# Linear attention into a two-expert mixture: places packed without a gap, and one tile at run-time offsets

## The chip, the cores and the metric

The kernel runs on one core of a Trainium2 chip. The metric is the device time of one execution in microseconds. Five engines work side by side on that core: TensorE (PE in the profile, PEld for its weight loads), VectorE (DVE), ScalarE (ACT), GpSimd (POOL) and SyncE (SP, which only issues transfers). The names PEq, PEldq, DVEq and so on are the instruction sequencers of these engines.

## What is computed

The reference, cut to what matters (8 batches, 8 heads, 576 tokens each, head width 64; so N = 4608 rows of D = 512; 8 experts with F = 1024; 2 modalities):

```python
q_s = softmax(q, axis=-1);  k_s = softmax(k, axis=2)
kv  = einsum('bhsd,bhse->bhde', k_s, v)
x   = einsum('bhsd,bhde->bhse', q_s, kv)      # then as N rows of D
logits = x @ w_gate + modality_bias[modality_id]
e_idx  = argmax(logits, axis=1)
gate_w = softmax(logits)[e_idx]
for e in range(E):
    mask = e_idx == e
    h = maximum(x[mask] @ w1[e], 0.0)
    out[mask] = gate_w[mask, None] * (h @ w2[e])
```

The inputs are one fixed draw. In it 2277 rows have modality 0 and 2331 have modality 1, and the expert that a row's argmax chooses is the one that its modality's bias favours.

## The kernel before

**Two experts are loaded, and rows are sorted by modality.** The kernel reads from the bias which expert each modality favours and loads the weights of these two alone into `W[:, 0]` and `W[:, 1]` (side A and side B). For each batch it loads q, k and v into a ring of five buffers `st`, takes exponentials (ACT), sums (DVE, L761), normalises q (mostly POOL, L777), builds `kv` on PE (L888) and from it a block-diagonal `kvbd` (DVE, L924), transposes q into the order of modalities on PE by a permutation matrix (L956, "s1"; the matrix `perm` comes from DVE, L806), multiplies by `kvbd` (L995, "s2"), and then copies windows of 64 columns into their places in `xs` (L1026, a "put", 18 of them per batch, on ACT, or on DVE for batches 2 and 5). Where a window starts is read at run time from running counts (`aoff`).

**Places.** `xs` holds NSLOT = 4864 places, 38 tiles of 128. Side A fills them from the left and side B from the right, each with up to CAP = 2432 places (19 tiles), so a gap is left between them. `lst`, `has` and `idx` hold the output row of each place, and `has` whether there is one.

**Passes.** For each side, seven passes run over fixed ranges of places (`passes_a`; `passes_b` mirrors them). A pass with number n may begin when batches 0 to n of its side have been put. Its widths are 256, 256, 256, 256, 512, 512 and 384 places. A pass computes the gates (logits on PE, L1060; bias and maximum on DVE, L1071 and L1072; exponentials on ACT, L1076), then for each of 8 blocks f of the hidden layer four matmuls (L1117, `h_mm`) and a relu (DVE L1093 or ACT L1091), and then for each tile eight matmuls of 512 columns (L1127, `y_mm`), a scaling by the gate (DVE L1099 or ACT L1097), and an indirect store of 128 rows on POOL (L1102).

**What sets the order.** A planner in the program (`Plan`) writes the instruction order of every engine ahead of time: a list scheduler with a cost and a rank for every step and rings of buffers (`r_ps` for seven PSUM banks, `r_st` for the loads). It runs at build time, so any step that is added, dropped or priced anew can shift the order of others. Up to 32 us it fills PE's gaps with matmuls that nothing reads (L1224).

**The general path.** After the planned part, `keys()` (L1240 to L1244) finds the expert of each place, a matmul counts the places whose expert is the expected one, and `ok` compares the running counts with what the passes assumed. If all hold, `nrest` is 0 and every engine skips a loop over all experts (branch at L1286, loop end at L1373) which would recompute everything. With this draw it is skipped. Its body begins with the logits and gates of all 38 tiles, so on PE it is long.

Of the kernel before, what the change touches and what calls it, by code (L numbers as in the profile page):

```python
# [232 lines left out]
def kernel(  # L233
# [44 lines left out]
    xs = sb([P, KD, NSLOT], BF16, "xs")  # L278
# [43 lines left out]
    def consts_pool(_):  # L322
# [11 lines left out]
        g.iota(kt_i, pattern=[[-64, NC]], base=NSLOT - 64, channel_multiplier=0)  # L334
# [281 lines left out]
    def vals_run(_):  # L616
# [4 lines left out]
        d.tensor_scalar(out=vals[:, :, 1], in0=idl, scalar1=1.0, scalar2=None, op0=ALU.add)  # L621

    def bsel_run(_):
# [5 lines left out]
        d.tensor_tensor(out=bsel, in0=bsel, in1=view(bias_b, [[0, NSL], [1, E]]), op=ALU.add)  # L629

# [53 lines left out]
    def idx_run(_):  # L684
# [27 lines left out]
    o_bsel = pl.op({"DVE": (1.17, 1.27, True)}, bsel_run, [o_off, o_exp], rank=11.5)  # L712
# [12 lines left out]
    def window(at, of_pass, T, last, right):  # L725

        lo, w = of_pass[1], of_pass[2]
        off = lo + (w - T) // 2
        if last:
            off = (lo if right else lo + w) - T // 2  # L730
# [3 lines left out]
            ap=[list(xs.ap[0]), [NSLOT, KD], [1, T]],  # L734
# [643 lines left out]
```

## Time and profile before

| | before |
|---|---|
| median of 3 runs | 215.15 us (214.55 to 215.34) |
| the profiled execution's own time | 213.42 us |
| its span in the profile | 211.7 us |
| mean granted TensorE clock | 0.974 of full speed |
| PE busy | 185.2 us (87%) |
| DVE busy | 155.4 us (73%) |
| ACT busy | 114.6 us (54%) |
| POOL busy | 97.2 us (46%) |

The time around the span is 213.42 - 211.7 = 1.72 us. The profiled execution lies 1.73 us below the median of the runs. Spans in the sections that follow are positions in the profiled execution, from the start of its span.

### The profile page before, as it was taken

Reading aid. Unit: us, or ns where it says so; the run is one execution under the profiler, and the core shown is the slowest. Engines: PE = TensorE matmul, PEld = TensorE weight load, DVE = VectorE, ACT = ScalarE, POOL = GpSimd, SP = SyncE. Lnnn points to the kernel's source line nnn. Section 1 sums busy time; section 2 is a strip of 40 time slices with the busy share of each in tenths; the row PEclk is TensorE's granted clock in tenths of the full one; section 3 lists DMA queues with packets and bytes.
Section 4 is the critical chain, followed back from the end, with each engine's and each line's share of the span. In section 5 each row is a group of like instructions: output and inputs, shape, how many; then the busy total and the mean of one; then the engine's idle time right before and its main releaser. Section 6 shows DMA issues by size and latency. Waiting matters only on the chain.

```text
span 211.7 us, 4660 instructions
## 1 busy us (share of the span) xinstructions
PE 185.2 (87%) x1587; PEld 110.4 (52%) x1587; DVE 155.4 (73%) x380; ACT 114.6 (54%) x313; POOL 97.2 (46%) x114
## 2 busy tenths in 40 slices
PE   3577959898978999999986999999999999999930
PEld 1234448487546585867653555554444444555520
DVE  3699798977679997887899977559757465566530
ACT  3528958989458599999797279959000000000000
POOL 3041950946933499767814937240150330505140
PEclk9999988999999999999999799999999999999996
DMA  6899999999999997999696100130031130312030
GB/s 193 290 398 392 212 184 215 281 370 297 292 412 411 403 397 229 366 374 376 186 405 249 50 3 0 51 125 29 0 150 51 50 148 0 149 53 89 0 116 5
DMA packets 20299, 42.35 MB, mean 200 GB/s; under 512 B 2607, under 2 KB 4655, under 8 KB 20272
## 3 DMA queue, kind: packets, MB, share of 16 engines
q1 hardware_dynamic: 13296, 28.33, 36.9%
q0 software_dynamic: 6304, 13.64, 23.2%
q8 instruction: 14, 0.23, 0.5%
q10 hardware_dynamic: 672, 0.05, 0.2%
q14 instruction: 13, 0.11, 0.2%
HBM read 36.76 MB, written 9.96 MB: 221 GB/s over the span
## 4 chain that ended last, share of the span: by engine, by line
PE 54%; DMA 21%; ACT 6%; DVE 6%; POOL 3%; issue 3%; SPq 2%; ACTq 0%; DVEq 0%; POOLq 0%
PE ps L1127 25%; PE ps L1117 23%; DMA W<-in_moe_w_dram 8%; DMA wg_f<-in_moe_w_gate_dram 5%; DMA st<-in_k_dram 4%; DMA st<-in_v_dram 4%; PE ps L956 2%; PE ps L888 2%; PE ps L1060 2%; ACT xs L1026 2%; ACT hT L1091 2%; PE ps L995 1%; ACT ex L1076 1%; DVE eq L777 1%; DVE own L761 1%
## 5 line engine op out<-in xcount | busy, mean ns | idle before, releaser
L1117 PE MATMUL ps<-xs,W 128*128 128x256 bf16 (+2 forms) x448 | 74.1, 317 | 1.9 <-ACT hT L1091 0.8
L1127 PE MATMUL ps<-W,hT 128*128 128x512 bf16 (+1 forms) x312 | 69.3, 374 | 1.8 <-DMA W<-in_moe_w_dram 1.2
L1102 POOL DMA_INDIRECT out_dram<-y_sb,idx x38 | 37.6, 990 | 68.9 <-DVE y_sb L1099 63.6
L1117 PEld LDWEIGHTS <-W 128*128 128x128 bf16 x448 | 43.4, 99 | 25.2 <-issue 4.9
L1127 PEld LDWEIGHTS <-hT 128*128 128x128 bf16 x312 | 30.0, 98 | 33.3 <-issue 2.1
L1099 DVE TENSOR_SCALAR y_sb<-ps,gate 128x512 f32<-128x512 f32 (+1 forms) x35 | 25.7, 734 | 27.2 <-PE ps L1127 23.5
L1093 DVE TENSOR_SCALAR hT<-ps 128x512 bf16<-128x512 f32 (+2 forms) x62 | 35.2, 576 | 7.0 <-PE ps L1117 4.9
L1026 ACT CAST xs<-ps 128x256 f32 (+1 forms) x108 | 32.8, 473 | 0.2 <-PE ps L995 0.2
L777 POOL TENSOR_TENSOR eq<-st,qi 128x512 bf16<-128x512 f32 (+1 forms) x30 | 28.3, 973 | 6.3 <-issue 3.2
L798 POOL CAST vb<-st 128x1152 bf16<-128x1152 f32 x14 | 15.8, 1146 | 18.5 <-DMA st<-in_v_dram 16.8
L761 DVE TENSOR_REDUCE own<-st 128x18 f32<-128x1152 f32 x16 | 21.6, 1352 | 2.9 <-ACT st L755 2.6
L755 ACT ACTIVATE st<-st 128x1152 f32<-128x1152 f32 x16 | 18.1, 1160 | 5.1 <-DMA st<-in_q_dram 5.1
L968 ACT CAST et<-ps 128x512 bf16<-128x512 f32 (+1 forms) x26 | 14.1, 573 | 12.1 <-PE ps L956 9.1
L1091 ACT ACTIVATE hT<-ps 128x256 bf16<-128x256 f32 (+1 forms) x50 | 18.7, 420 | 2.9 <-PE ps L1117 2.8
L788 ACT ACTIVATE ek<-st 128x1152 bf16<-128x1152 f32 x16 | 18.5, 1184 | 2.7 <-DMA st<-in_k_dram 2.7
L1076 ACT ACTIVATE ex<-L,gmx 128x8 f32<-128x8 f32 x38 | 11.5, 303 | 7.7 <-DVE gmx L1072 6.9
L956 PE MATMUL ps<-perm,eq 128*128 128x128 bf16 x144 | 13.6, 229 | 2.2 <-DVE eq L777 2.0
L888 PE MATMUL ps<-vb,ek 64*128 64x129 bf16 x288 | 11.4, 217 | 4.5 <-POOL vb L798 2.9
L1224 PE MATMUL ps<-ones 128*128 128x512 bf16 x43 | 13.5, 473 | 1.2 <-POOL ones L324 1.2
L888 PEld LDWEIGHTS <-ek 64*128 64x128 bf16 x288 | 8.7, 93 | 9.4 <-issue 7.0
L956 PEld LDWEIGHTS <-eq 128*128 128x128 bf16 x144 | 9.9, 102 | 6.6 <-DVE eq L777 3.0
L1026 DVE CAST xs<-ps 128x256 f32 x36 | 12.2, 417 | 0.0
(106 smaller groups left out, 142.1 us busy)
## 6 DMA issues: line engine op xcount, KB each, us to landing
st<-in_q_dram SPq DMA_DIRECT2D x7, 1152.0 KB, 11.4
st<-in_k_dram SPq DMA_DIRECT2D x7, 1152.0 KB, 13.8
st<-in_v_dram SPq DMA_DIRECT2D x7, 1152.0 KB, 10.4
W<-in_moe_w_dram POOLq DMA_DIRECT2D x8, 256.0 KB
W<-in_moe_w_dram POOLq DMA_DIRECT2D x4, 512.0 KB
st<-in_q_dram SPq DMA_DIRECT2D x2, 576.0 KB, 5.8
st<-in_k_dram SPq DMA_DIRECT2D x2, 576.0 KB, 8.1
st<-in_v_dram SPq DMA_DIRECT2D x2, 576.0 KB
```

What stands on the lines that cost most here:

```text
L761: nc.vector.tensor_reduce(out=sums[qib.idx][:, h * NJ : (h + n) * NJ], in_=view(st[bq.idx], [[Dh, n * NJ], [1, Dh]], h * NJ * Dh), op=ALU.add,
L777: (nc.vector if e == "DVE" else nc.gpsimd).tensor_tensor(out=view(eq[eqb.idx], [[HG * Dh, n], [Dh, HG], [1, Dh]], j0 * HG * Dh), in0=view( ...
L788: nc.scalar.activation(out=view(ek[ekb.idx], [[Dh, n], [HG * Dh, NJ], [1, Dh]], h * Dh), in_=view(st[bk.idx], [[NJ * Dh, n], [Dh, NJ], [1, ...
L888: nc.tensor.matmul(out=ps_t[kvp[hg].idx][:, 130 * hp : 130 * hp + 129], lhsT=ek[ekb.idx][rows, j, P * hp : P * hp + P], rhs=vb[vbb.idx][ro ...
L956: nc.tensor.matmul(out=view(t, [[2 * nj * 64, 2], [1, 64]], hp * nj * 64 + jj * 64), lhsT=eq[eqb.idx][:, j0 + jj, P * hp : P * hp + P], rh ...
L1026: w_ = nc.scalar.copy(out=dst, in_=src) if e == "ACT" else nc.vector.tensor_copy(out=dst, in_=src)
L1091: nc.scalar.activation(out=dst, in_=src, func=ACT.Relu)
L1093: nc.vector.tensor_scalar_max(out=dst, in0=src, scalar1=0.0)
L1099: nc.vector.tensor_scalar(out=dst, in0=src, scalar1=g, scalar2=None, op0=ALU.mult)
L1102: s_ = nc.gpsimd.indirect_dma_start(out=out, out_offset=bass.IndirectOffsetOnAxis(ap=ix[:, c : c + 1], axis=0), in_=ysb, in_offset=None, b ...
L1117: nc.tensor.matmul(out=t[:, 0:w], lhsT=W[:, slot_, kd * F + f * P : kd * F + (f + 1) * P], rhs=xs[:, kd, lo : lo + w], start=(kd == 0), st ...
L1127: nc.tensor.matmul(out=t, lhsT=h[:, kf, i * P : (i + 1) * P], rhs=W[:, slot_, W2 + kf * D + c0 : W2 + kf * D + c0 + cn], start=(kf == 0), ...
```

## The change

Places are packed: `xs` has exactly N = 4608 places, 36 tiles, with no gap; the middle is MID = 2304, after 18 tiles. The fixed passes cover 18 tiles on each side, the last one with 256 places instead of 384. The tile in which the larger side runs over the middle holds rows of both sides; the fixed pass of the smaller side's expert runs over it too, and the rows of the wrong side there get an output index out of bounds. One more tile, the **rest**, goes over it again with the larger side's expert (`ffn_rest`). Which tile it is and which expert is known only at run time: `mid_run` (DVE) computes `over`, the patched indices and `idx_x`; ACT reads two registers (`load_at`), copies the tile out of `xs` (`copy_x`, 128x512) and copies one expert's weights out of `W` into two `st` buffers in four pieces of 128x2048 bf16 (`copy_w`). Then PE runs 32 matmuls of 128 columns (`h_rest`) and 8 of 512 (`y_rest`).

Since the sides touch, the passes with n = 7 wait for the puts of both sides (`whole`, `final`), and the last put of a batch on one side follows the other's (`across`). The digits that `hlo` keeps in `xs` early on move to place 3*S. `ok` gets a further pair of limits: the larger side may not run over the middle by more than one tile (2176 <= count <= 2432 for side A). The general path loses the gates of all tiles in its outer body and computes them tile by tile in the inner loop.

The diff, cut to its core:

```diff
-    CAP = 2432
-    NSLOT = 2 * CAP
-    NSL = NSLOT // P
+    NSL = N // P
+    MID = N // 2
+    TM = MID // P
     GW = 512
-    passes_a = [(0, 0, 256), (1, 256, 256), (2, 512, 256), (3, 768, 256), (5, 1024, 512), (7, 1536, 512), (7, 2048, 384)]
-    passes_b = [(n, NSLOT - lo - w, w) for n, lo, w in passes_a]
+    passes_a = [(0, 0, 256), (1, 256, 256), (2, 512, 256), (3, 768, 256), (5, 1024, 512), (7, 1536, 512), (7, 2048, 256)]
+    passes_b = [(n, N - lo - w, w) for n, lo, w in passes_a]
...
-        a = CAP - HC // 8 * P + (c % (HC // 4)) * P
+        a = 3 * S + (c % (HC // 4)) * P
...
-        d.tensor_scalar(out=has, in0=lst[:, 1, :], scalar1=0.5, scalar2=None, op0=ALU.is_ge)
         d.scalar_tensor_tensor(
             out=lst[:, 0, :], in0=lst[:, 0, :], scalar=64.0, in1=lst[:, 1, :], op0=ALU.mult, op1=ALU.add
         )
+        d.tensor_copy(out=idx, in_=lst[:, 0, :])
+    def mid_run(_):
+        d = nc.vector
+        two, rest = lst[:, 0, TM - 1 : TM + 1], isb[:, TM - 1 : TM + 1]
+        d.tensor_scalar(out=over[:, 0:1], in0=aoff[:, NC : NC + 1], scalar1=MID + 0.5, scalar2=None, op0=ALU.is_ge)
+        d.tensor_scalar(out=over[:, 1:2], in0=over[:, 0:1], scalar1=-1.0, scalar2=1.0, op0=ALU.mult, op1=ALU.add)
+        d.tensor_copy(out=over_i, in_=over[0:1, :])
+        d.scalar_tensor_tensor(out=both[:, 0, :], in0=rest, scalar=OOB, in1=two, op0=ALU.mult, op1=ALU.add)
+        d.scalar_tensor_tensor(out=both[:, 1, :], in0=rest, scalar=-OOB, in1=two, op0=ALU.mult, op1=ALU.add)
+        d.tensor_scalar_add(out=both[:, 1, :], in0=both[:, 1, :], scalar1=OOB)
+        d.tensor_copy(out=idx[:, TM - 1 : TM], in_=both[:, 0, 0:1])
+        d.tensor_copy(out=idx[:, TM : TM + 1], in_=both[:, 1, 1:2])
+        d.tensor_scalar(out=both[:, 1, 0:1], in0=both[:, 1, 0:1], scalar1=over[:, 1:2], scalar2=None, op0=ALU.mult)
         d.scalar_tensor_tensor(
-            out=lst[:, 1, :], in0=lst[:, 0, :], scalar=-OOB, in1=has, op0=ALU.add, op1=ALU.mult
-        )
-        d.tensor_scalar_add(out=idx, in0=lst[:, 1, :], scalar1=OOB - 1.0)
...
+    o_bsel = pl.op({"DVE": (1.25, 1.35, True)}, bsel_run, [o_off, o_exp], rank=11.5)
+    o_mid = pl.op({"DVE": (1.0, 1.15, True)}, mid_run, [o_idx, o_bsel], rank=41)
...
+        n, lo, w = of_pass
+        off = lo + (w - T) // 2 if n < B - 1 else MID - T // 2
...
+                        if b == B - 1:
+                            final.append(w_)
                     before = win[-2] if len(win) > 1 else filled[b - 1][side - 2] if b else None
+                    across = win[-1 - 2 * side] if j0 + jj == NJ - 1 else None
...
+                if whole and not i and not c:
+                    for w_ in final[-2:]:
+                        sync(m, w_, "every batch is in its places")
...
+        whole = n == B - 1
+        deps = [o for b in range(n + 1) for o in filled[b][0 if whole else side :: 1 if whole else 2]]
...
+    def ffn_rest(gs, rank):
+        def load_at(_):
+            at.extend(
+                nc.values_load_multi_w_load_instructions(
+                    over_i[0:1, 0:2],
+                    engines=[ENG.Activation],
+                    min_val=0,
+                    max_val=1,
+                    skip_runtime_bounds_check_because=WHY,
+                )[1]
+            )
+        def copy_x(_):
+            nc.scalar.copy(
+                out=xx,
+                in_=bass.AP(
+                    tensor=xs.tensor,
+                    offset=xs.offset + (at[0] * P + (MID - P)),
+                    ap=[list(xs.ap[0]), [N, KD], [1, P]],
+                    dep_tracking_offset=xs.offset + MID - P,
+                ),
+            )
+        def copy_w(i):
+            def run(_):
+                n = WSZ // 4
+                nc.scalar.copy(
+                    out=wx(i // 2)[:, (i % 2) * n : (i % 2 + 1) * n],
+                    in_=W[:, bass.ds(at[1], 1), i * n : (i + 1) * n],
+                )
+            return run
+        def h_rest(i, fb):
+            def run(_):
+                for f in range(4):
+                    for kd in range(KD):
+                        nc.tensor.matmul(
+                            out=ps_t[fb.idx][:, f * P : (f + 1) * P],
+                            lhsT=wx(0)[:, kd * F + (4 * i + f) * P : kd * F + (4 * i + f + 1) * P],
+                            rhs=xx[:, kd, :],
+                            start=(kd == 0),
+                            stop=(kd == KD - 1),
+                        )
+            return run
+        def y_rest(fb):
+            def run(_):
+                for kf in range(KF):
+                    nc.tensor.matmul(
+                        out=ps_t[fb.idx],
+                        lhsT=hT[hb.idx][:, kf, 0:P],
+                        rhs=wx(1)[:, kf * D : (kf + 1) * D],
+                        start=(kf == 0),
+                        stop=(kf == KF - 1),
+                    )
+            return run
...
+        la = pl.op({"ACT": (0.6, 0.7)}, load_at, [o_mid], rank=94)
+        xc = pl.op(on_act(KD * P), copy_x, [la, *deps], rank=96)
+        wc = []
+        for i in range(4):
+            wc.append(
+                pl.op(
+                    on_act(WSZ // 4),
+                    copy_w(i),
+                    [la, *w_in[0], *w_in[1], *(x for nm in "qkv" for x in loads[nm, B - 1][0])],
+                    rank=97 + i,
+                    takes=[] if i % 2 else [wb[i // 2]],
+                    uses=[wb[i // 2]] if i % 2 else [],
+                )
+            )
...
+        ym = pl.op(
+            on_pe(*[D] * KF), y_rest(fb), [*hs, *wc], rank=500 + rank + 0.2, takes=[fb], uses=[hb, wb[1]]
+        )
...
+        pl.op(
+            {"POOL": (1.05, 3.8)}, lambda _: store(0, y_sb[yb.idx], idx_x, "stores"), [ye, o_mid], rank=-1, uses=[yb]
+        )
...
+        gs = [ffn(side, *p, rank=2.0 * i + side) for side, p in enumerate((pa, pb))]
+    ffn_rest(gs, 2.0 * i + 0.7)
...
-    early = sorted({(n, lo + w) for n, lo, w in passes_a if n < B - 1})
+    early = sorted({(n, lo + w) for n, lo, w in passes_a if n < B - 1}) + [(B - 1, MID - P)]
...
-        for t0 in range(0, NSL, 19):
-            logits(t0, 19, ps_t[1])
-            gates1(t0, 19, ps_t[1])
-            gates2(t0, 19)
-            gates3(t0, 19)
-        keys()
-        nc.vector.tensor_scalar(out=sel, in0=kk, scalar1=kcol, scalar2=None, op0=ALU.is_equal)
-        nc.vector.tensor_tensor(out=sel, in0=sel, in1=has, op=ALU.mult)
-        nc.vector.scalar_tensor_tensor(
-            out=sel, in0=lst[:, 0, :], scalar=-OOB, in1=sel, op0=ALU.add, op1=ALU.mult
-        )
-        nc.vector.tensor_scalar_add(out=ixe, in0=sel, scalar1=OOB - 1.0)
...
+            d.tensor_copy(out=xx, in_=xs[:, :, bass.ds(c * P, P)])
+            d.tensor_copy(out=b1, in_=bsel[:, bass.ds(c, 1), :])
+            d.tensor_copy(out=l1, in_=lst[:, 0, bass.ds(c, 1)])
+            for kd in range(KD):
+                nc.tensor.matmul(
+                    out=ps_t[4][:, 0:E], lhsT=xx[:, kd, :], rhs=wg_sb[:, kd, :], start=(kd == 0), stop=(kd == KD - 1)
+                )
+            d.tensor_tensor(out=b1, in0=ps_t[4][:, 0:E], in1=b1, op=ALU.add)
```

The order that the planner gives moves in many places. Two matter for what follows.

DVE around the puts of batch 5 (window copies `xs<-ps`), before. `kvbd` is that of batch 5, `own<-st` is the sum of q of batch 6 (two instructions of 18 sums), `y_sb` is the scaling of a pass tile:

```order
L924 TENSOR_TENSOR kvbd_75<-ps_95,kinv_89 64x2x64 x2
L924 TENSOR_TENSOR kvbd_75<-ps_94,kinv_89 64x2x64 x2
L761 TENSOR_REDUCE own<-st_65 128x18 x2
L1099 TENSOR_SCALAR y_sb_84<-ps_92,gate 128x512
L1026 REGISTER_ALU
L1026 ISA
L1026 COPY xs<-ps_93 128x4x64
```

The same place on DVE, changed. `perm` is the permutation matrix of batch 7, and `hT` a relu:

```order
L951 TENSOR_TENSOR kvbd_75<-ps_94,kinv_89 64x2x64 x2
L951 TENSOR_TENSOR kvbd_75<-ps_95,kinv_89 64x2x64 x2
L833 TENSOR_TENSOR perm_79<-own,posx 128x1152
L1120 TENSOR_SCALAR hT_81<-ps_93 128x256
L1053 REGISTER_ALU
L1053 ISA
L1053 COPY xs<-ps_91 128x4x64
```

The sum of q of batch 6 and the scaling no longer stand between `kvbd` and the first put; the sum comes right behind the last put. The matrix of batch 7, which before had been built ahead of `kvbd`, and one relu now stand between.

PE at the end of the planned part, before, up to the first rows of the general path. L1286 is the branch that skips it:

```order
L1253 LDWEIGHTS ones
L1253 MATMUL ps_90<-cnt_b,ones 128x1
L1285 TENSOR_LOAD nrest
L1286 COMPARE_AND_BRANCH
L1286 UNCONDITIONAL_BRANCH x2
L1373 BRANCH_PREFETCH_HINT
L1060 LDWEIGHTS xs
L1060 MATMUL ps_91<-wg_sb,xs 128x8
```

The same on PE, changed. The branch is L1451, and L1483 is the inner loop over tiles:

```order
L1416 LDWEIGHTS ones
L1416 MATMUL ps_90<-cnt_b,ones 128x1
L1450 TENSOR_LOAD nrest
L1451 COMPARE_AND_BRANCH
L1451 UNCONDITIONAL_BRANCH x2
L1541 BRANCH_PREFETCH_HINT
L1483 COMPARE_AND_BRANCH
L1483 UNCONDITIONAL_BRANCH x2
```

The logits of all tiles are gone from behind the branch. On PE the skip is row 3176 of 3572 before and row 3208 of 3308 after, so 396 rows stood behind it, and now 100.

## Rows read from the trace of the kernel before

**Rows 1.** Windows: stretch, its length, busy time by engine, granted clock, DMA share, GB/s.

```profile
60.20:109.90 49.70, 48.92 (x520) 34.77 (x519) 42.83 (x97) 43.67 (x111) 31.97 (x32) 1.00 0.95 352
109.90:118.10 8.20, 4.66 (x83) 2.98 (x80) 8.13 (x24) 5.37 (x6) 3.69 (x4) 1.00 0.58 223
118.10:122.60 4.50, 4.50 (x48) 2.23 (x45) 3.63 (x15) 2.27 (x10) 4.49 (x5) 0.62 0.15 58
122.60:203.10 80.50, 79.99 (x500) 41.31 (x497) 52.66 (x99) 21.74 (x85) 25.77 (x28) 1.00 0.16 60
...
150.00:212.00 62.00, 53.09 (x271) 26.30 (x269) 33.34 (x57) 0.00 (x0) 17.70 (x18) 0.97 0.18 69
```

**Rows 2.** Timeline of PE in the stall: start, us, work, count [idle before, releaser].

```profile
111.64 0.67 PE L888 MATMUL ps<-vb,ek 64*128 64x129 bf16 x17 [1.51 <-DVE y_sb L1099]
...
116.43 0.69 PE L888 MATMUL ps<-vb,ek 64*128 64x129 bf16 x18 [0.96 <-POOL vb L798]
117.53 0.69 PE L888 MATMUL ps<-vb,ek 64*128 64x129 bf16 x18 [0.41 <-POOL vb L798]
```

**Rows 3.** Timeline of DVE in the same stretch.

```profile
104.42 1.35 DVE L806 TENSOR_TENSOR perm<-own,posx 128x1152 bf16<-128x1152 f32 x1
...
106.74 1.20 DVE L924 TENSOR_TENSOR kvbd<-ps,kinv 64x128 bf16<-64x128 f32 x4
107.97 2.83 DVE L761 TENSOR_REDUCE own<-st 128x18 f32<-128x1152 f32 x2
...
111.50 6.04 DVE L1026 CAST xs<-ps 128x256 f32 x18
117.46 0.18 DVE L772 TENSOR_SCALAR qi<-own 128x36 f32<-128x36 f32 x1
```

**Rows 4.** Timeline of POOL, 96 to 120 us.

```profile
96.92 4.68 POOL L777 TENSOR_TENSOR eq<-st,qi 128x512 bf16<-128x512 f32 x5 [1.11 <-ACT xs L1026]
...
115.23 2.24 POOL L798 CAST vb<-st 128x1152 bf16<-128x1152 f32 x2 [2.40 <-DMA st<-in_v_dram]
```

**Rows 5.** Chain of work that ended last: start, us, what, count.

```profile
87.01 0.44 PE ps L1117 x4
...
100.44 0.22 PE ps L956 x4
...
106.59 8.49 DMA st<-in_v_dram
...
118.21 0.91 PE ps L1060 x32
...
156.40 6.91 PE ps L1117 x32
...
183.60 5.20 PE ps L1117 x32
188.80 5.18 PE ps L1127 x24
...
197.88 4.34 PE ps L1127 x24
```

**Rows 6.** Instructions of L1286: duration ns min/median/max, first and last start.

```profile
L1286 DVEq COMPARE_BRANCH  x3: 41/51/61, 204.8 to 207.5; - x3
L1286 PEldq COMPARE_BRANCH  x3: 101/192/3753, 204.9 to 210.4; - x3
```

**Rows 7.** Instructions of L1373, the end of the program, same columns.

```profile
L1373 POOLq DRAIN  x3: 46/103/286, 207.5 to 211.5; - x3
...
L1373 PEldq DRAIN  x2: 8/8/8, 210.6 to 210.9; - x2
```

**Rows 8.** DMA queues, 205 to 210.5 us: packets, MB, share.

```profile
q8 instruction: 2, 0.03, 3.2%
```

**Rows 9.** Costliest groups: busy, mean ns, idle before.

```profile
L788 ACT ACTIVATE ek<-st 128x1152 bf16<-128x1152 f32 x16 | 18.5, 1184 | 2.7 <-DMA st<-in_k_dram 2.7
```

**Rows 10.** The page's DMA queues over the whole span, columns as in rows 8.

```profile
q8 instruction: 14, 0.23, 0.5%
```

More of the change, by code (lines that the diff above doesn't have):

```diff
@@ L456 @@
     eid_i = sb([1, 2], I32, "eid_i")
+    keyd = sb([P, 1], FP32, "keyd")
     krow = sb([P, NSL], FP32, "krow")
@@ L543 @@
     lst = sb([P, 2, NSL], FP32, "lst")
-    has = sb([P, NSL], FP32, "has")
     idx = sb([P, NSL], I32, "idx")
+    both = sb([P, 2, 2], FP32, "both")
+    over = sb([P, 2], FP32, "over")
+    over_i = sb([1, 2], I32, "over_i")
+    idx_x = sb([P, 1], I32, "idx_x")
+    gate_x = sb([P, 1], FP32, "gate_x")
+    xx = sb([P, KD, P], BF16, "xx")
     bsel = sb([P, NSL, E], FP32, "bsel")
@@ L722, with window @@
         load_batch(b)
[L725 to L730, printed above, removed]
+    def window(at, of_pass, T):
+        n, lo, w = of_pass
+        off = lo + (w - T) // 2 if n < B - 1 else MID - T // 2
         return bass.AP(
@@ L733, in window, with sync @@
             offset=xs.offset + at,
-            ap=[list(xs.ap[0]), [NSLOT, KD], [1, T]],
+            ap=[list(xs.ap[0]), [N, KD], [1, T]],
             dep_tracking_offset=xs.offset + off,
+        )
+    final = []
+    def sync(later, first, reason):
+        tc.add_manual_dep(
+            later.ins,
+            first.ins.name,
+            mybir.DependencyInfo(mybir.DependencyClass.Sync, mybir.DependencyReason.DATA),
+            reason=reason,
         )
@@ L1055, with logits @@
     gate = sb([P, NSL], FP32, "gate")
-    def logits(t0, nt, t):
+    def logits(t0, nt, t, whole=False):
         for i in range(nt):
             for c in range(KD):
-                nc.tensor.matmul(
+                m = nc.tensor.matmul(
                     out=t[:, i * E : (i + 1) * E],
@@ L1123, in h_mm @@
             )
+            if whole and not f and not kd:
+                for w_ in final[-2:]:
+                    sync(m, w_, "every batch is in its places")
     def y_mm(t, h, i, slot_, c0=0, cn=D):
@@ L1141, in ffn @@
             on_pe(*[32] * (nt * KD)),
-            lambda _: logits(t0, nt, ps_t[gb.idx]),
+            lambda _: logits(t0, nt, ps_t[gb.idx], whole),
             deps + [wg_c],
@@ L1205, in ffn @@
                 lambda _, i=i, yb=yb: store(t0 + i, y_sb[yb.idx], idx, "stores"),
-                [*evs, o_idx],
+                [*evs, o_idx, o_mid if whole else None],
                 rank=-1,
@@ L1212, in ffn, with wx, gate_rest @@
             pl.op({"POOL": (3.0, 3.0)}, lambda _: nc.gpsimd.drain(), [st_], rank=-1)
+        return g3
+    def ffn_rest(gs, rank):
+        deps = [o for b in range(B) for o in filled[b]]
+        wb, hb, at = [Buf(r_st), Buf(r_st)], Buf(r_hT), []
+        def wx(i):
+            return st[wb[i].idx].bitcast(BF16)
+        def load_at(_):
[49 more added lines that the diff above has]
+            return run
+        def gate_rest(_):
+            d = nc.vector
+            d.tensor_scalar(
+                out=gate_x, in0=gate[:, TM - 1 : TM], scalar1=over[:, 1:2], scalar2=None, op0=ALU.mult
+            )
+            d.scalar_tensor_tensor(
+                out=gate_x, in0=gate[:, TM : TM + 1], scalar=over[:, 0:1], in1=gate_x, op0=ALU.mult, op1=ALU.add
+            )
+        g = pl.op({"DVE": (0.2, 0.35)}, gate_rest, [*gs, o_mid], rank=95)
+        la = pl.op({"ACT": (0.6, 0.7)}, load_at, [o_mid], rank=94)
[12 more added lines that the diff above has]
+            )
+        hs = []
+        for i in range(2):
+            fb = Buf(r_ps)
+            hm = pl.op(
+                on_pe(*[P] * (4 * KD)),
+                h_rest(i, fb),
+                [xc, *wc[:2]],
+                rank=500 + rank,
+                takes=[fb] if i else [fb, hb],
+                uses=[wb[0]],
+                lag=0.5,
+            )
+            hs.append(
+                pl.op(
+                    {**on_act(4 * P), **on_dve(4 * P)},
+                    lambda e, i=i, fb=fb: relu(
+                        e,
+                        hT[hb.idx][:, 4 * i : 4 * i + 4, 0:P],
+                        ps_t[fb.idx].rearrange("p (f n) -> p f n", f=4),
+                    ),
+                    [hm],
+                    rank=-1,
+                    uses=[fb, hb],
+                )
+            )
+        fb, yb = Buf(r_ps), Buf(r_y)
+        ym = pl.op(
+            on_pe(*[D] * KF), y_rest(fb), [*hs, *wc], rank=500 + rank + 0.2, takes=[fb], uses=[hb, wb[1]]
+        )
+        ye = pl.op(
+            {**on_dve(D), **on_act(D + 100)},
+            lambda e: scaled(e, y_sb[yb.idx], ps_t[fb.idx], gate_x),
+            [ym, g],
+            rank=-1,
+            takes=[yb],
+            uses=[fb],
+        )
+        pl.op(
+            {"POOL": (1.05, 3.8)}, lambda _: store(0, y_sb[yb.idx], idx_x, "stores"), [ye, o_mid], rank=-1, uses=[yb]
+        )
```

63 lines of the change are left out of this document (31 added, 32 removed).

## The prediction

> **What bounds the kernel now.** I read the windows first, since shares over the whole span mix stages. From 60.2 to 109.9 us PE is busy 48.92 of 49.70, and from 122.6 to 203.1 it is busy 79.99 of 80.50, both at full clock [rows 1]. In these two stretches the time is PE's work, and only fewer or shorter matmuls help. [...] PE waits 1.51 us for a scaling on DVE, and 0.96 and 0.41 for the cast of v of batch 7 on POOL [rows 2]. DVE first sums q of batch 6 (107.97, 2.83 us) and only then, from 111.50 to 117.54, puts batch 5 [rows 3], for which the next logits wait; they start at 118.21 [rows 5]. That v of batch 7 is late itself: its transfer runs from 106.59 for 8.49 us [rows 5], behind a long normalisation on POOL at 96.92 [rows 4].
>
> The chain of waits then shows the last passes as one unbroken run of PE [rows 5]. It ends at 202.2, yet the program ends at 211.7. The instructions at the end explain some of that: the skip of the general path takes PE's sequencer up to 3753 ns and no other engine over 61 [rows 6], and PE reaches its last drain at 210.6 where POOL does at 207.5 [rows 7].
>
> **The change part by part.** The sum is made against the profiled execution's own 213.42 us, which is 1.73 below the median; I carry differences over to the median.
>
> *1. Fewer columns on PE.* A matmul of 384 columns takes 5.20/32 = 0.1625 us, one of 512 columns 5.18/24 = 0.216, one of 256 columns 0.44/4 = 0.110, and one of 128 columns with weights of its own 0.22/4 = 0.055 [rows 5]. Before, the last passes have 2 x 32 of 384 columns and 6 tiles of 8: 64 x 0.1625 + 48 x 0.216 = 20.77 us. Now they have 64 of 256, 4 tiles of 8, and the rest with 32 of 128 and 8 of 512: 7.04 + 6.91 + 1.76 + 1.73 = 17.44. The difference is 3.33. Two tiles of logits go as well, 8 matmuls of 0.91/32 = 0.028, 0.23 us. Nothing hides beside PE there, so all of it counts: **-3.6**. The 55 ns come from runs of four to eight, and the rest has runs of 16; if weight loads limited it, the price would go toward that of 256 columns, 32 x 0.110 = 3.52, and the term would be -1.8.
>
> [...]
>
> *2. The branch.* Instructions come to PE in packets: 14 packets [rows 10] for 3572 rows are 255 rows each. While PE stands at the branch, two such packets are moved [rows 8]. The branch had 396 rows to skip, more than a packet, and now 100. So the target should be in a packet that PE has, or the next one, and the 3.75 us should shrink to the 0.06 of other engines. What is late next is POOL's drain at 207.5, so 210.6 - 207.5 = 3.1 us at most goes, less what PE still needs: **-2.8**. The ends are 0, if the target still has to be fetched, and -3.3.
>
> [...]
>
> *3. The hole in the middle.* In the changed order DVE goes from `kvbd` of batch 5 to `perm` (1.35 us [rows 3]), one relu and then the puts; the sum and a scaling, 2.83 us and more, come later. `perm` no longer stands ahead of `kvbd`, which so ends some 1.35 us before 107.9. The first put then begins near 108.3 and the last ends near 114.3, 3.2 us before 117.54. On PE the first half of `kv` of batch 7 moves behind the logits (0.91) and four groups of 512-column matmuls (16 x 0.216 = 3.5), so it is reached near 118.7, after the cast (115.23 to 117.47 [rows 4]). The waits of 0.96 and 0.41 should go wholly, and of the 1.51 [rows 2] some two thirds, since the scalings now stand ahead of `kvbd` on DVE. That is **-2.4**. The ends: nothing, if something else in the new order is late; and all 3.54 us idle plus the slow clock's 4.50 x 0.38 = 1.7, so -5.2. I count the clock as unchanged.
>
> *4. What is added.* `mid_run` is 10 small DVE instructions at no more than 0.18 [rows 3], 1.8 us; the index step loses two and the gates one. They fall in the stretch where DVE is 86% busy [rows 1], mostly in its gaps. `load_at` makes ACT wait for `mid_run` and read two registers; behind it on ACT queue windows and exponentials of the next batches. The four weight copies cost 4 x 2048 x 1184/1152 ns = 8.4 us [rows 9] and `copy_x` 0.5; ACT does nothing after 150 us [rows 1] and the rest is needed after 183, so they cost nothing (8.9 us if that cover were gone, part of it ahead of exponentials whose gates are wanted near 151). The wait of the n = 7 passes for both sides costs nothing: PE enters the last 512-column passes at 156.40 [rows 5], long after the last puts. The count's small instructions on DVE are now in one block among the relus, up to 1.2 us by seven rows like those of 0.18. Ends 0 and +2.5; I take **+0.6**.
>
> Sum: -3.6 - 2.8 - 2.4 + 0.6 = -8.2. That is 205.2 for an execution like the profiled one, and 215.15 - 8.2 = **207.0 us** as a median.
>
> **The rivals.** *A. The hole stays* (another wait takes its place). For it: DVE is 8.13 of 8.20 busy there [rows 1], and reordering doesn't take work off it; the sum of q of batch 6 still has to come. Against it: the logits don't need that sum. Terms 1, 2 and 4 remain, -5.8: 209.4. *B. The branch stays slow*, because the fetch is forced by any taken branch, or for another reason than code. For it: the stall is seen once, and its cause is inferred from two packets. Terms 1, 3 and 4 remain, -5.4: 209.8. *Both stay:* -3.0, 212.2. *C. Both ends of term 3 are won*, hole and clock: 204.2. *D. Slower: v of batch 7 arrives much later.* The new order puts `perm` and a relu of batch 6's time ahead of the reciprocal that the long POOL normalisation (96.92) waits for. That instruction's buffer is what the load of q of batch 7 needs, and behind it on SP's queue stands v of batch 7 (106.59 plus 8.49, then the cast). `kv` of batch 7 is on PE in front of everything after it. About 1.5 us more (one `perm`, 1.35, and a part of a relu) is covered by the 118.7 against 117.5 of term 3; the time passes 215.15 only if the delay is over 8.2 + 1.2 = 9.4 us, which needs a whole further transfer (8.49) to come in front: then 215.2 + and above, 216. *E. The change doesn't do what it says:* the new limit fails and the general path runs, hundreds of us. The count of modality 0 is 2277, within 2176 to 2432, so only an expert other than the favoured one could bring it about, as before.
>
> **How the numbers follow.** The forecast has 0.48, A 0.20, B 0.09, both 0.06, C 0.10, D 0.04, E 0.03. From 204.0 to 211.0 lie the forecast, A, B and nearly all of C, with the bounds of term 4 (0 to 2.5) and of `h_rest` (1.8) around them; outside are "both", D, E and the edge of C, less than 0.2. A measurement of this kernel can tell about 0.5% from no change, 1.1 us. All cases but D and E are faster by more than that. Faster 0.92; same 0.03 from "both" with the dear `h_rest`; slower 0.05.
>
> **What would show it.** Step 1: the chain of the last passes has 32-matmul pieces near 3.5 us, and `h_rest` near 0.9 per 16. Step 2: PE's branch at or under 0.2 us and its drain beside the others'; if it is 3 us or more, B. Step 3: the last put of batch 5 near 114, the logits right behind, PE's idle time between 109 and 119 near 1 us instead of 3.5, and a short or no stretch of low clock; if PE is idle for 3 us or more, A. Step 4: ACT's copies over before 165, and no wait of PE for `xx` or `st`. The prediction is wrong at its root if the planner's other moves, in the 50 us before the hole, open a wait of PE in a stretch that is now 98% full.

## The result, and the profile after

The changed kernel takes 207.59 us (median of 4 runs, 205.45 to 209.32) where the kernel before, with one run more on the same chip, takes 214.85 (4 runs). The ratio is 0.9635, with a 95% interval of 0.9541 to 0.973. Here and below, medians are of all runs, while ratios and their intervals are of the runs within 1.5% of their kernel's fastest, which leaves out the 209.32. The forecast was 207.0 in a range of 204.0 to 211.0. The profiled execution takes 205.45 us with a span of 203.7, 7.97 us below that of before.

The windows of the changed kernel (stretch, its length, busy time of PE, PEld, DVE, ACT and POOL, granted clock, DMA share, GB/s), to be held against [rows 1]:

```profile
57.00:108.90 51.90, 50.47 (x541) 35.22 (x541) 43.60 (x107) 44.14 (x113) 32.84 (x33) 1.00 0.95 341
108.90:114.50 5.60, 4.89 (x57) 2.61 (x57) 5.60 (x18) 5.60 (x7) 0.98 (x1) 1.00 1.03 407
114.50:122.00 7.50, 7.50 (x91) 4.09 (x92) 7.16 (x18) 7.04 (x18) 5.16 (x5) 1.00 0.25 94
...
129.00:141.80 12.80, 10.48 (x122) 6.30 (x120) 6.78 (x14) 11.97 (x30) 4.37 (x5) 1.00 0.22 84
141.80:198.20 56.40, 56.33 (x327) 30.25 (x323) 35.97 (x70) 12.98 (x37) 15.49 (x16) 1.00 0.17 66
```

The hole of 109.9 to 118.1, in which PE idled 3.54 us before [rows 1], is nearly closed: PE idles 0.71 us between 108.9 and 122, and the clock stays full there. But a new one has opened, from 129 to 141.8, where PE idles 2.32 us and ACT is busy 11.97 of 12.80. DVE and PE at the old hole, from the timeline of the changed kernel (start, us, work, count, idle before and its releaser), beside [rows 2, 3]:

```profile
107.11 1.36 DVE L833 TENSOR_TENSOR perm<-own,posx 128x1152 bf16<-128x1152 f32 x1
...
108.72 6.05 DVE L1053 CAST xs<-ps 128x256 f32 x18
...
114.48 0.85 PE L1084 MATMUL ps<-wg_sb,xs 128*128 128x8 bf16 x28 [0.70 <-DVE xs L1053]
...
140.47 1.36 PE L1084 MATMUL ps<-wg_sb,xs 128*128 128x8 bf16 x48 [1.92 <-ACT xs L1053]
```

And PE at the logits of n = 5 before:

```profile
118.14 0.97 PE L1060 MATMUL ps<-wg_sb,xs 128*128 128x8 bf16 x32
```

The copies of batch 5 begin at 108.72 instead of 111.50, and the logits that wait for them at 114.48 instead of 118.14. Yet the logits of n = 7 begin at 140.47, hardly earlier than before. The chain of the kernel before there, with the first piece of matmuls behind them and the last scaling:

```profile
140.83 1.33 PE ps L1060 x54
...
142.57 6.93 PE ps L1117 x32
...
203.12 0.48 DVE y_sb L1099
```

What the logits of n = 7 wait for in the changed kernel is ACT's window copies of batches 6 and 7. ACT's timeline, changed kernel:

```profile
125.66 6.54 ACT L1053 CAST xs<-ps 128x256 f32 x16
...
132.34 8.08 ACT L1053 CAST xs<-ps 128x256 f32 x20
140.31 1.90 ACT L1279 COPY st<-W 128x2048 bf16 x1
...
148.13 5.50 ACT L1279 COPY st<-W 128x2048 bf16 x3
```

And before:

```profile
128.99 5.08 ACT L1026 CAST xs<-ps 128x256 f32 x18
...
134.30 5.24 ACT L1026 CAST xs<-ps 128x256 f32 x18
```

Before, 36 copies take 10.32 us, 0.29 each. Now they take 14.62 us, 0.41 each. ACT starts 3.3 us earlier (125.66 against 128.99) and ends 0.9 us later (140.42 against 139.54). The last three weight copies, by contrast, end at 153.6, long before they are needed.

The chain of waits in the changed kernel (start, us, what, count), beside [rows 5]: first the last copy on ACT, then the passes. L1290 is `h_rest`, L1303 `y_rest`:

```profile
140.05 0.38 ACT xs L1053
...
141.83 6.06 PE ps L1144 x28
...
184.19 0.89 PE ps L1290 x16
...
190.74 1.73 PE ps L1303 x8
...
194.65 3.47 PE ps L1157 x24
198.17 0.47 DVE y_sb L1126
```

The instructions at the end (duration ns min/median/max, first and last start), beside [rows 6, 7]; L1451 is the branch, L1541 the program's end:

```profile
L1451 PEldq COMPARE_BRANCH  x3: 101/187/310, 199.9 to 202.7; - x3
...
L1541 POOLq DRAIN  x3: 46/103/204, 202.6 to 203.5; - x3
...
L1541 PEldq DRAIN  x2: 8/8/8, 202.9 to 203.2; - x2
```

PE's branch takes 0.31 us instead of 3.75, and PE reaches its drain at 202.9, 0.3 us behind POOL. The branches of the other engines take at most 0.06 us, as before [rows 6].

So the 7.97 us between the two profiled executions part like this. From the end of the last scaling to the end of the span it was 211.7 - 203.6 = 8.1 us and is 203.7 - 198.64 = 5.06: 3.0 gained. From the start of the logits of n = 7 to the last scaling it was 203.6 - 140.83 = 62.8 and is 198.64 - 140.47 = 58.2: 4.6 gained. Of these, 0.86 are four matmuls of 512 columns that PE now has behind it at that point, which belong to the stretch before; the rest, 3.7, is the fewer columns and logits. The stretch up to there gives 0.36 + 0.86 = 1.2. Part of what it gains is hidden in this pair of executions: the changed kernel's started later, since POOL issues the last weights at 44.02 and not at 42.56 (lines under "The order in the middle"). Over all profiled runs that point lies anywhere from 42.56 to 45.10. Measured from it, the stretch gives 1.2 + 1.46 = 2.7.

### The profile page after: what moved, and what is told of

Its sections match the earlier page's. It is cut to its first block, busy times and chain, and to the rows that moved or that the text cites. A ratio compares the mean times of both kernels' runs of the same rounds, so it can differ in the third digit from the quotient of the medians.

```text
span 203.7 us, 4709 instructions
## 1 busy us (share of the span) xinstructions
PE 179.5 (88%) x1603; PEld 110.5 (54%) x1603; DVE 153.9 (76%) x385; ACT 129.5 (64%) x323; POOL 94.0 (46%) x111
## 4 chain that ended last, share of the span: by engine, by line
PE 48%; ACT 16%; DVE 12%; DMA 9%; issue 6%; POOL 4%; SPq 2%; DVEq 0%; ACTq 0%; POOLq 0%
PE ps L1157 22%; PE ps L1144 19%; ACT xs L1053 7%; DMA wg_f<-in_moe_w_gate_dram 5%; DMA st<-in_k_dram 4%; DVE own L788 4%; ACT hT L1118 3%; ACT ex L1103 2%; DVE xs L1053 2%; PE ps L915 2%; POOL eq L804 2%; ACT ek L815 1%; POOL out_dram L1129 1%; DVE kvbd L951 1%; DVE eq L804 1%
## 5 line engine op out<-in xcount | busy, mean ns | idle before, releaser
L1144 PE MATMUL ps<-xs,W 128*128 128x256 bf16 (+1 forms) x448 | 69.3, 304 | 0.9 <-ACT et L995 0.2
L1129 POOL DMA_INDIRECT out_dram<-y_sb,idx x36 | 35.6, 990 | 68.8 <-DVE y_sb L1126 48.5
L1157 PE MATMUL ps<-W,hT 128*128 128x512 bf16 (+1 forms) x296 | 65.8, 373 | 1.1 <-ACT y_sb L1124 0.5
L1118 ACT ACTIVATE hT<-ps 128x256 bf16<-128x256 f32 (+1 forms) x55 | 21.6, 458 | 39.0 <-PE ps L1144 31.0
L1157 PEld LDWEIGHTS <-hT 128*128 128x128 bf16 x296 | 28.2, 98 | 31.0 <-issue 1.6
L1126 DVE TENSOR_SCALAR y_sb<-ps,gate 128x512 f32<-128x512 f32 (+1 forms) x29 | 21.2, 731 | 24.4 <-PE ps L1157 20.6
L1053 ACT CAST xs<-ps 128x256 f32 (+1 forms) x108 | 35.9, 443 | 1.1
L1120 DVE TENSOR_SCALAR hT<-ps 128x256 bf16<-128x256 f32 (+1 forms) x59 | 31.8, 545 | 5.4 <-PE ps L1144 4.1
L825 POOL CAST vb<-st 128x1152 bf16<-128x1152 f32 x12 | 14.2, 1200 | 16.8 <-DMA st<-in_v_dram 16.5
L995 ACT CAST et<-ps 128x512 bf16<-128x512 f32 (+1 forms) x24 | 12.5, 559 | 9.7 <-PE ps L983 9.6
```

Of the source, the lines that this page charges most:

```text
L1053: w_ = nc.scalar.copy(out=dst, in_=src) if e == "ACT" else nc.vector.tensor_copy(out=dst, in_=src)
L1118: nc.scalar.activation(out=dst, in_=src, func=ACT.Relu)
L1120: nc.vector.tensor_scalar_max(out=dst, in0=src, scalar1=0.0)
L1126: nc.vector.tensor_scalar(out=dst, in0=src, scalar1=g, scalar2=None, op0=ALU.mult)
L1129: s_ = nc.gpsimd.indirect_dma_start(out=out, out_offset=bass.IndirectOffsetOnAxis(ap=ix[:, c : c + 1], axis=0), in_=ysb, in_offset=None, b ...
L1144: m = nc.tensor.matmul(out=t[:, 0:w], lhsT=W[:, slot_, kd * F + f * P : kd * F + (f + 1) * P], rhs=xs[:, kd, lo : lo + w], start=(kd == 0) ...
```

## Experiments

All runs are given with the median of the kernel before that ran on the same chip in between.

| kernel | us | before | ratio, 95% interval |
|---|---|---|---|
| changed kernel again | 207.20 | 213.39 | 0.9714 (0.9633 to 0.9794) |
| e1: copies tracked by side | 202.90 | 213.39 | 0.9517 (0.9433 to 0.9600) |
| e3: skip of 388 rows | 210.64 | 213.39 | 0.9854 (0.9802 to 0.9905) |
| e4: before, skip of 92 rows | 210.28 | 213.39 | 0.9826 (0.9712 to 0.9939) |
| e2: before, copies at one spot | 218.54 | 213.72 | none given |
| e5: before, sum late | 216.06 | 213.72 | 1.0106 (1.0061 to 1.0150) |
| e8: before, both orders | 213.25 | 213.72 | 0.9948 (0.9919 to 0.9977) |
| e6: changed, sum early | 214.11 | 213.72 | 1.0032 (0.9995 to 1.0069) |
| e7: e1 without the rest | 202.48 | 213.28 | 0.9510 (0.9432 to 0.9587) |
| e10: skip of 300 rows | 209.83 | 213.28 | 0.9809 (0.9716 to 0.9902) |
| e11: e7 without a drain | 199.60 | 213.91 | 0.9363 (0.9307 to 0.9419) |
| e12: skip of 196 rows | 207.19 | 213.91 | 0.9688 (0.9632 to 0.9744) |

### Why ACT's copies became slower

In the changed kernel `window` gives all copies of batches 6 and 7, of both sides, one tracked place around the middle. Whatever their real addresses, each is then taken to overwrite the one before it. Before, the two sides had a place each and took turns. **e1_split** gives them places of their own again; only the very last pair, whose windows can really overlap, is tracked across the middle:

```diff
-        off = lo + (w - T) // 2 if n < B - 1 else MID - T // 2
+        off = lo + (w - T) // 2 if n < B - 1 else MID - T // 2 if last else MID - T + side * T
...
-                        dst = window(a, p, 64)
+                        dst = window(a, p, 64, side, c == NC - 1)
```

> The changed kernel with one edit: the window copies of batches 6 and 7 are tracked beside the middle, side A left and side B right of it, and only the last pair of all across it; the order of instructions on every engine is that of the changed kernel. Theory 1 (in the changed kernel all these copies are tracked at one spot, so each waits for the one before it to be written): the copies on ACT go from 0.40 us each back to 0.29 as before the change, the last ends near 136.5 instead of 140.3, PE's idle time between 129 and 142 us falls from 2.3 to under 1 us, and the time falls by 1.5 to 2.3 us, to 205.3 to 206.1. Rival (the copies take 0.40 us for another reason, such as memory shared with other engines): 0.40 us stays, and the time is that of the changed kernel, 207.1 to 208.1.

The timeline of e1 (ACT, then PE) and its window:

```profile
125.57 4.55 ACT L1053 CAST xs<-ps 128x256 f32 x16
...
130.31 6.06 ACT L1053 CAST xs<-ps 128x256 f32 x20
...
137.63 1.34 PE L1084 MATMUL ps<-wg_sb,xs 128*128 128x8 bf16 x48
...
129.00:141.80 12.80, 12.70 (x125) 7.19 (x122) 8.76 (x22) 12.13 (x42) 4.46 (x5) 1.00 0.22 84
```

The copies take 10.61 us again, the last ends at 136.4, and PE's idle time falls from 2.32 to 0.10 us. The theory holds, the rival falls. The gain, 4.3 us against the changed kernel on the same chip, is larger than the 1.5 to 2.3 that I expected. **after_again**, the changed kernel beside it, shows the rest.

> The changed kernel itself, on the chip of the other three, to compare them with: 205.5 to 209.3 as before, branch of PE 0.3 us, last copy of batch 7 on ACT at 140.3.

Its windows, up to the start of n = 7 and just behind it:

```profile
129.00:141.10 12.10, 9.78 (x108) 5.62 (x106) 6.07 (x13) 11.31 (x29) 3.96 (x4) 1.00 0.23 89
141.10:148.90 7.80, 7.80 (x33) 3.21 (x30) 6.60 (x22) 7.41 (x31) 0.00 (x0) 0.78 0.01 2
```

In this execution PE idles 2.32 us in 12.10, and then runs 7.80 us at a granted clock of 0.78: by my estimate 7.80 x 0.22 = 1.7 us more. The 28 matmuls of 512 columns right behind the logits of n = 7 bear it out: they take 7.89 us here and 6.20 in the first profile of the same kernel. In that first profile the clock stayed at 1.00. That profile is the exception: e3, e10 and e12 below have the same hole, and in their profiles the granted clock of the 7 to 8 us behind it is 0.78, 0.76 and 0.59. So the new hole costs 2.3 us, and in four of the five profiles with it an estimated 1.7 to 3.1 more (7.0 x 0.24 = 1.7 in e10, 7.5 x 0.41 = 3.1 in e12); e1 has no hole, and no such stretch.

**e2_before_one_spot** does the same thing to the kernel before: one tracked place for the last batches, and the wait for both sides.

```diff
-            off = (lo if right else lo + w) - T // 2
+            off = CAP - T // 2
...
+                if whole and not i and not c:
+                    sync(m)      # waits for the last copies of both sides
```

> The kernel before with one thing of the change alone: the window copies of batches 6 and 7 of both sides are tracked at one spot, and the passes with n = 7 wait for the last copies of both sides. Theory 1 (copies tracked at one spot wait for each other): ACT's 36 copies go from 0.29 to 0.40 us each, the last ends near 143.5 instead of 139.5, PE waits some 3 us for it ahead of the logits of n = 7, perhaps with a stretch of low clock behind (up to 1.8 us), and the time rises by 2.5 to 5 us over the kernel before. Rival (the 0.40 us have another cause, or ACT has room): the time of the kernel before within 0.7 us.

ACT and PE in its timeline:

```profile
129.25 7.33 ACT L1037 CAST xs<-ps 128x256 f32 x18
136.96 7.27 ACT L1037 CAST xs<-ps 128x256 f32 x18
...
144.29 1.56 PE L1074 MATMUL ps<-wg_sb,xs 128*128 128x8 bf16 x56 [1.69 <-ACT xs L1037]
```

0.41 us each, the end at 144.2, as expected. How much time this costs is less sure: the four runs take 215.16 to 218.88 us, 1.4 to 5.2 above the 213.72 of before, where 2.5 to 5 were expected. Much of that spread goes with the clock: the fastest run has a mean granted clock of 0.977, the others 0.954 to 0.964, and in the profiled one it is 0.78 in the 7.7 us behind the wait. With e1 this shows the cause of the slow copies from both sides.

### The branch

**e4_before_short_skip** leaves the logits' matmuls out of the general path of the kernel before, **e3_long_skip** puts 288 such rows into that of the changed kernel. The planned part is untouched in both.

```diff
 e4, in the general path of the kernel before:
-            logits(t0, 19, ps_t[1])
 e3, in the general path of the changed kernel:
+        for t0 in range(0, NSL, 18):
+            logits(t0, 18, ps_t[1])
```

> The kernel before without the logits' matmuls in the body of the general path, which this draw does not enter (the general path would be wrong there): PE's skip is 92 rows instead of 396, and the planned part is the same. Theory: PE's branch falls from 3.75 to about 0.3 us, PE drains with the other engines, and the time falls by 2.7 to 3.3 us from 214.85, to 211.6 to 212.2. Rival: it stays at 3.75 us and 214.3 to 215.4.

> The changed kernel with the logits of all 36 tiles put back at the head of the general path's body: 288 rows on PE that are never executed, so that PE's skip is 388 rows long instead of 100. The planned part is the same. Theory (the long wait at the branch is for code, because the target lies beyond the packets that PE holds): PE's branch takes 3 to 4 us, its last drain comes 2.5 to 3.3 us behind the other engines', the time rises by 2.5 to 3.3 us, to 210.1 to 210.9. Rival (the wait went for another reason that the change brought, such as where the program ends): the branch stays at 0.3 us and the time at 207.1 to 208.1.

The branch of PE in e4:

```profile
L1286 PEldq COMPARE_BRANCH  x3: 101/187/310, 204.2 to 207.1; - x3
```

And in e3:

```profile
L1451 PEldq COMPARE_BRANCH  x3: 101/196/3707, 201.3 to 206.7; - x3
```

The wait comes and goes with rows that are never executed: by the medians -3.1 us in e4 against the kernel before, +3.4 in e3 against the changed one. Two more kernels ask which length decides. They put the logits of 25 and of 12 tiles there:

```diff
 e10:
+        logits(0, 25, ps_t[1])
 e12:
+        logits(0, 12, ps_t[1])
```

> The changed kernel with the logits of 25 tiles at the head of the general path's body: 200 rows on PE that are never executed, so the skip is 300 rows long, more than a packet of 255, and the loop's end is at row 3508, which lies in the packet behind that of the branch (row 3208) if packets are counted by 256 from the first row. Theory (what counts is whether the target lies in the packet of the branch or the next): PE's branch takes 0.3 us and the time is that of the changed kernel within 0.7 us. Rival (a skip longer than one packet waits): 3 to 4 us at the branch and 2.5 to 3.5 us more time, as in e3_long_skip.

> The changed kernel with the logits of 12 tiles at the head of the general path's body: the skip on PE is 196 rows long, less than a packet of 255, and ends at row 3404. Theory of length (a skip shorter than one packet finds its target in the packet at hand or the next): the branch takes 0.3 us, and the time is that of the changed kernel within 0.7 us. Rival (the target is not there although it is near, since what counts is where the packets begin): 3 to 4 us at the branch and 2.5 to 3.5 us more.

PE's branch in e10:

```profile
L1451 PEldq COMPARE_BRANCH  x3: 97/196/3727, 203.0 to 208.4; - x3
```

PE's branch in e12:

```profile
L1451 PEldq COMPARE_BRANCH  x3: 101/187/310, 202.1 to 204.8; - x3
```

The lines of the instruction queue q8 on the pages of e10 and of e12 (packets, MB, share), beside [rows 10]:

```profile
q8 instruction: 14, 0.23, 0.4%
```

```profile
q8 instruction: 13, 0.21, 0.4%
```

The skip of 196 rows takes PE 0.31 us, as that of 100 does; the skip of 300 makes it wait the full 3.73 us. (The time of e10, 209.28 to 211.11 us in three runs and 207.34 in one, is too scattered to size it: its interval overlaps that of the changed kernel.) The queue agrees with the reading that the wait is for code: q8 moves 14 packets in every run in which PE's branch takes 3.6 us or more (before, e2, e3, e5, e8, e10), and 13 in every run in which it takes 0.31 (the changed kernel, its repeat, e1, e4, e6, e7, e11, e12). That q8 feeds PE is inferred from these counts. My theory for e10, that a target in the packet behind that of the branch is at hand, fell, at least with packets counted from the first row. Whether the length alone decides, or a border of packets between rows 3404 and 3508, stays open.

### The order in the middle

**e5_before_sum_late** makes one of the two moves in the kernel before, on DVE; **e8_before_both_orders** also puts kv of batch 7 behind the logits on PE; **e6_sum_early** takes DVE's move back in the changed kernel.

```diff
 e5 and e8, the kernel before:
-                    [e] + sq,
+                    [e] + sq + (filled[5][-1:] if b == 6 else []),
 e8 alone:
+        if n == 5:
+            pl.later(kvs[7][0], lg)
 e6, the changed kernel:
+        if b == 6:
+            for o in filled[5][:2]:
+                pl.later(o, sq[-1])
```

> The kernel before with the sum of q of batch 6 planned behind the window copies of batch 5 on DVE; PE keeps its order, in which all of kv of batch 7 stands ahead of the logits. Theory of the two orders: the copies end near 115.2 instead of 117.5, but PE still stands at kv of batch 7 until the cast of v at 117.5, so the hole stays, and the time is that of the kernel before within 0.8 us. Rival (DVE's order alone makes the hole): PE idles 1 us instead of 3.5 and the time falls by 2 to 3.5 us.

> The kernel before with both moves of order and nothing else of the change: the sum of q of batch 6 behind the window copies of batch 5 on DVE, and kv of batch 7 behind the logits of n = 5 on PE. Its ACT copies of batches 6 and 7 still take 0.29 us each. Theory of the two orders: the logits begin near 115.4 instead of 118.2, PE's idle time between 109 and 119 falls from 3.5 to about 1 us, the clock stays full, and the time falls by 2.5 to 4.5 us. Rival (what is won there is given back at the copies of batch 7, or the hole reopens elsewhere): the time falls by less than 1 us.

> The changed kernel with the sum of q of batch 6 and one scaling put ahead of the window copies of batch 5 on DVE again, as before the change (the planner then also puts kv of batch 7 half ahead of the logits). Theory: the copies start 3.6 us later, near 112.3, and end near 118.3; the hole reopens, PE idles 3 us or more between 109 and 119, and the copies of batches 6 and 7, which set PE's start into n = 7, end 2 to 3 us later; the time rises by 2 to 4 us over the changed kernel. Rival (ACT's slow copies set the end of this stretch anyway): within 0.7 us of the changed kernel.

e5, timeline of PE and one window:

```profile
118.29 2.25 PE L888 MATMUL ps<-vb,ek 64*128 64x129 bf16 x36 [3.34 <-POOL vb L798]
...
119.00:130.00 11.00, 11.00 (x95) 5.76 (x91) 7.29 (x19) 5.44 (x23) 6.28 (x8) 0.74 0.07 25
```

e8, the same:

```profile
117.77 0.86 PE L1061 MATMUL ps<-wg_sb,xs 128*128 128x8 bf16 x28 [1.62 <-DVE xs L1027]
...
119.00:130.00 11.00, 11.00 (x85) 5.39 (x84) 10.57 (x28) 7.76 (x26) 9.84 (x11) 0.84 0.07 25
```

e6, timeline of PE, then one line of ACT's:

```profile
117.98 1.15 PE L918 MATMUL ps<-vb,ek 64*128 64x129 bf16 x18 [4.01 <-ACT ek L815]
119.07 1.02 PE L1087 MATMUL ps<-wg_sb,xs 128*128 128x8 bf16 x32
...
145.21 0.95 PE L1087 MATMUL ps<-wg_sb,xs 128*128 128x8 bf16 x32 [1.82 <-ACT xs L1056]
```

```profile
115.71 1.15 ACT L825 CAST vb<-st 128x1152 bf16<-128x1152 f32 x1 [1.96 <-DMA st<-in_v_dram]
```

DVE's move alone doesn't help: PE stands 3.34 us at kv of batch 7 instead, the clock is low for longer (0.74 over 11 us), and the kernel is 2.3 us slower, where I expected no change. Both moves together give 0.5 us by the medians and 1.1 by the ratio, less than the 2.5 to 4.5 expected: the logits still wait 1.62 us for DVE, and the slow clock (0.84 over 11 us, by estimate 11.00 x 0.16 = 1.8 us) is not gone. e6 takes 6.8 us more than the changed kernel (ratio 1.0032 against 0.9714), where 2 to 4 were expected. But it undoes more than DVE's move. Half of kv of batch 7 (18 of 36 matmuls) is back ahead of the logits, and PE stands 4.01 us at it, for ACT's exponential of k, which ACT reaches only behind a cast that waits for v; the logits begin at 119.07. So the hole comes back in full, but e6 doesn't show what DVE's order alone is worth. As the planner is free to move other steps too, these three runs are less clean than e1 and e2.

The lead of the changed kernel at the logits of n = 5 is larger than in e8. These executions differ by up to 2.4 us in when POOL issues the last weights, so I measure from there. POOL's timeline in the kernel before, e8 and the changed kernel, one line each:

```profile
42.56 1.55 POOL L495 DMA_DIRECT2D W<-in_moe_w_dram  x2
```

```profile
44.99 1.56 POOL L495 DMA_DIRECT2D W<-in_moe_w_dram  x2
```

```profile
44.02 1.55 POOL L494 DMA_DIRECT2D W<-in_moe_w_dram  x2
```

From these to the logits it is 118.14 - 42.56 = 75.6 us before, 117.77 - 44.99 = 72.8 in e8, and 114.48 - 44.02 = 70.5 in the changed kernel. In e8 and the changed kernel PE has 36 matmuls of kv, 1.4 us, still to do at that point, so that much of either lead is work put off and not won. So the two moves make 2.8 of 5.1 us; the other 2.3 come from further moves in the 50 us before, which I did not take apart.

### What the rest tile costs

**e7_split_no_rest** is e1 without `ffn_rest`: the 27 rows of the larger side that run over the middle are left out.

```diff
-    ffn_rest(gs, 2.0 * i + 0.7)
```

> The kernel of e1_split without the rest tile: the rows of the larger side that run over the middle are not computed (27 rows of the output are left out), and with it go the register loads, the four weight copies and the tile's copy on ACT, 40 matmuls, two relus, one scaling and one store. Theory of the sum (PE's matmuls are all that the rest costs, 32 x 0.055 + 8 x 0.216 = 3.5 us, and ACT's copies are hidden): 3.3 to 3.8 us below e1_split, a ratio to the kernel before near 0.935. Rival (the 8.9 us of ACT's copies, the register loads or the relus cost something too): 4.5 us or more below e1_split.

The time falls by 0.4 us only. POOL's last store in e1, and in e7:

```profile
196.07 0.98 POOL L1129 DMA_INDIRECT out_dram<-y_sb,idx  x1 [0.50 <-DVE okm L1436]
```

```profile
195.74 0.98 POOL L1129 DMA_INDIRECT out_dram<-y_sb,idx  x1 [2.77 <-issue]
```

What stands ahead of it in e7, the drains of POOL's queue (ns min/median/max, first and last start):

```profile
L1243 POOLq DRAIN  x5: 3125/3784/5204, 137.9 to 191.8; - x5
```

PE's last matmuls of y run to 192.7, in e1 to 195.3. Measured from the issue of the last weights (44.45 here, 43.47 in e1) that is 3.6 us earlier than in e1. But a drain that the kernel puts behind the last pass of side A now starts at 191.8, takes over 3 us, and the last store stands behind it. **e11_no_rest_no_drain** takes that drain out.

```diff
-        if n >= 5 and not last:
+        if n >= 5 and lo + w != MID and lo != MID:
```

> The kernel of e7_split_no_rest (no rest tile, 27 rows of the output left out) without POOL's drain behind the last pass of side A. In e7_split_no_rest PE ended 3.5 us earlier than in e1_split, measured from the issue of the last weights, but that drain of 3 to 4 us then stood ahead of the last store, which came only 0.3 us earlier. Theory (the rest costs PE 3.5 us, and the drain took the gain): the last store starts within 1 us of PE's end, and the time is 2 to 3.5 us below e7_split_no_rest, a ratio to the kernel before of 0.934 to 0.942. Rival (another limit stands at the same place, such as the store itself): the ratio stays at 0.95.

POOL's last store in e11:

```profile
192.50 0.98 POOL L1129 DMA_INDIRECT out_dram<-y_sb,idx  x1 [0.50 <-DVE y_sb L1126]
```

199.60 us, a ratio of 0.9363 against 0.9517 of e1: 0.0154 x 213.4 = 3.3 us for the rest. So it costs about its matmuls on PE (3.5 us expected), and ACT's 8 us of copies cost nothing. e11 lacks the drain as well as the rest; that the drain itself costs e1 nothing is read from e1's trace, where the last store waits for DVE. It becomes the end only in e7, where PE gets shorter.

## Why the prediction was right, and where it was not

**Fewer columns: right.** 3.6 us forecast, 3.7 read between the profiles. `h_rest` takes 0.89/16 = 0.056 us a matmul in its runs of sixteen, close to the 0.055 of [rows 5] for batches of four.

**The branch: right, by a part of its reason.** 2.8 forecast; 3.0 between the profiles, 3.1 and 3.4 in e4 and e3. That the wait is for code has support: it came and went with rows that are never executed, and with a 14th packet. The size of the packet told the right side of the limit; the finer rule, "the packet that PE has, or the next", did not stand in e10.

**The hole in the middle: the mechanism right, its gain mostly lost.** The copies begin at 108.72 (forecast 108.3), end at 114.77 (114.3), the logits follow at 114.48, PE idles 0.7 us, the clock stays full. By the starts alone that is 3.7 us, more than the 2.4 I took. But at 140.5 only 1.2 us of it are left. (Measured from the last weights it is 5.1 and 2.7; either way 2.4 are lost between.)

**What is added: the step that failed.** I wrote that the wait of the n = 7 passes for both sides costs nothing, since PE enters "the last 512-column passes" at 156.40, long after the last copies. But a pass begins with its logits, and on the chain of the kernel before those of n = 7 stand at 140.83, 1.3 us behind the last copy. (156.40 is late even for the 512-column matmuls: of the 152 of L1117 behind 140.83 the passes with n = 7 need 128, so by count theirs begin within the piece at 142.57.) The cover was 1.3 us, not 17. In that place the change puts a new cost that I had read in the diff (`MID - T // 2` for both sides) without asking what it does to the copies themselves: 36 x 0.12 = 4.3 us on ACT. What the cover did not hide shows as 2.3 us of idle PE, where e1 has 0.10. It took the extra gain of the hole, and in four of five profiled executions more, through the clock, which I had counted as unchanged. The small things that I did price, `mid_run`, `load_at`, the count's block, do not show in the passes: PE is busy 56.33 of 56.40 us behind 141.8.

Against the profiled executions the terms were -3.6, -2.8 and -1.8 (the middle with its extras), and came out as -3.7, -3.0 and -1.2, the last being -2.7 with 1.5 of later start against it. Against medians the middle is smaller still: in the second comparison the whole is 213.39 - 207.20 = 6.2 us, of which columns and branch (3.7 and 3.1) are already more. So the forecast of 207.0 came close because a larger gain in the hole and a cost that I had missed nearly cancelled. Rivals A and B did not come about as I had put them, though the middle ends near A's outcome: by the medians almost nothing is left of its gain, for the hole moved 20 us on. That the sum came so near owes its middle part to luck.

**e1 beats both kernels:** 202.90 us, a ratio of 0.9517 to the kernel before and 4.3 us below the changed one.

## What to carry to other kernels

When a change alters where a write is tracked, and not only where it goes, look at the engine that makes the writes: here a chain of false overlaps added 0.12 us to each, and showed as a group whose mean rose from 0.29 to 0.41 us while its shape stayed the same. Before an edit is costed at nothing, name the first instruction that needs its result, not the first long one. And code that never ran had a price here, too: 3.4 us by the medians for 388 rows that a branch at the very end leaps over, where 196 rows cost nothing that shows (207.19 us in e12, 207.20 in the changed kernel again).

## What was not expected of the hardware

A window copy of 128x256 on ACT took 0.29 us in the kernel before and in e1, and 0.41 us in the changed kernel and in e2, where it is tracked as one that overwrites the copy before it. PE's branch took 0.31 us over 92, 100 and 196 rows (e4, the changed kernel, e12) and 3.71 to 3.75 us over 300, 388 and 396 (e10, e3, before), while all other engines took at most 0.06 us at theirs. An idle time of 2.3 us out of 12, at most 1.9 of it in a row, was followed by a clock of 0.78 in one execution of a kernel and by 1.00 in another.
